# Sliding-window decode attention on one core: two engines' written-out orders become loops, transposes move ahead of the spread, the last values get banks of their own, and the last load is cut anew

## The chip, the cores and the metric

The kernel runs on one core of one Trainium2 chip. The metric is the device time of one execution in microseconds (us). Before the change the median of three runs is 183.75 us (183.66 to 183.91). The profiled execution, which all durations here come from, took 183.87 us, of which its span, from the first to the last instruction, is 182.6 us.

## The reference, cut to what matters

```python
B, Sq, D = 32, 1, 512;  Hq, Hkv, Sk, Dh = 32, 8, 2048, 128     # all bfloat16
W = 512                                   # the last 512 of 2048 cached positions
q = (x @ wq).reshape(B, Sq, Hq, Dh).transpose(0, 2, 1, 3)
k = repeat(k_cache[:, :, Sk - W:, :], 4, axis=1)                # each kv head serves 4 q heads
v = repeat(v_cache[:, :, Sk - W:, :], 4, axis=1)
p = softmax(einsum("bhqd,bhkd->bhqk", q, k) * Dh ** -0.5)
o = einsum("bhqk,bhkd->bhqd", p, v)
return o.transpose(0, 2, 1, 3).reshape(B, Sq, Hq * Dh) @ wo
```

Per core: 33.5 MB of keys, 33.5 MB of values and two weights of 4.2 MB are read, 75.5 MB in all, and 32 KB are written.

## The kernel before

The 32 batch rows are worked through in eight **quads** of four, numbered 0 to 7. One quad's keys (or values) are 4 MB, laid on 128 partitions, 32 KB on each; a partition is one (row, kv head, quarter of the window). Two buffers each hold keys (`K_sb`) and values (`V_sb`).

Every step has a letter, a quad and sometimes a part; the orders are written out with these names at the top of the file:

- **T** (VectorE, L516): transposes a quad's keys into `KT_sb`, in two halves, T.0 and T.1.
- **S** (TensorE, L346): the scores, half S.0 from T.0 and half S.1 from T.1.
- **M** (VectorE, L522 and L524): the maximum, negated. **X** (ScalarE, L565): the exponential with its sums. **N** (VectorE, L528 and L530): reciprocal and scaling, into `P_bf`.
- **E** (TensorE, L360): turns the probabilities to the layout of the values. **G** (ScalarE, L572): copies them out of PSUM into `PTc`.
- **B** (VectorE L536, ScalarE L578): the *spread*, `PTc` times a mask into `bd`, once for each of eight kv heads, shared out between the two engines.
- **P** (TensorE, L372): `bd` against the values, 32 groups of four matmuls, into four banks of PSUM, `O_ps`; "P7.0.18" is quad 7's groups 0 to 17.
- **C** (VectorE L541, ScalarE L583): *picks* four blocks out of those banks into `C_sb`. **F** (TensorE, L382) *folds* them, and **D** (ScalarE, L586) copies the fold into `o_sel`.
- **W** (TensorE, L467): `o_sel` times wo, 32 blocks, then two small copies and two stores.

What sets the order: each engine runs its steps in the written order (TensorE with a loop over three rounds of two quads, L440; VectorE and ScalarE unrolled, `DVE_OPS` and `ACT_OPS`), and `needs` gives each step the steps of other engines that it waits for. A P needs its spread, and the pick of the quad before, since `O_ps` is one set of banks. An N needs the X before it; an E needs its N. A fold F needs its pick. SyncE issues all loads in the order of `LOADS`; before a load into a buffer that is in use it waits for the T (keys, L250) or the pieces of P (values, L257) that read it last. wo goes into `K_sb` in three loads, W0, W1 and W2 (L265), of 22, 8 and 2 of its 32 blocks.

Around the change the order of the end is this:

```python
TAIL_OPS = "P7.0.18 P7.18.32 F6 F7"
DVE_OPS  = "... T6.0 M5 T6.1 N5 B5.0.4 C4.2.4 M6 T7.0 N6 T7.1 B6.0.4 C5.2.4 M7 N7 B7.0.5 C6.2.4 C7.2.4"
WOP      = [(0, 22), (22, 30), (30, 32)]
```

Of the kernel before, what the change touches and what calls it, by code (L numbers as in the profile page):

```python
# [19 lines left out]
S0.0 S0.1 S1.0 S1.1 E0 E1 P0.0.32  # L20
# [6 lines left out]
P7.0.18 P7.18.32 F6 F7  # L27
"""
ROUNDS = 3
DVE_OPS = """  # L30
T0.0 T0.1 T1.0 M0 T1.1 N0 M1 N1 B0.0.4 B1.0.4 T2.0 T2.1 M2 N2 B2.0.4 T3.0 T3.1 M3 N3 B3.0.4 T4.0
T4.1 M4 N4 B4.0.4 T5.0 C3.2.3 T5.1 C3.3.4 T6.0 M5 T6.1 N5 B5.0.4 C4.2.4 M6 T7.0 N6 T7.1 B6.0.4
C5.2.4 M7 N7 B7.0.5 C6.2.4 C7.2.4
"""
ACT_OPS = """
X0 X1 G0 B0.4.8 G1 B1.4.8 C0.0.4 X2 D0 G2 B2.4.8 C1.0.4 X3 D1 G3 B3.4.8 C2.0.4 X4 D2 G4 B4.4.8
C3.0.2 X5 D3 G5 B5.4.8 C4.0.2 X6 D4 G6 B6.4.8 C5.0.2 X7 D5 G7 B7.5.8 C6.0.2 C7.0.2 D6 D7
"""
# [7 lines left out]
WOP = [(0, 22), (22, 30), (30, 32)]  # L46

# [5 lines left out]
def bass_standalone__sliding_block_cached__sampling_kernel(  # L53
# [22 lines left out]
    NG = 4  # L76
# [7 lines left out]
    orders = {"PE": head + sum(rounds, []) + tail, "DVE": ops_of(DVE_OPS), "ACT": ops_of(ACT_OPS)}  # L84

    ends, total = {}, {}
    for eng, ops in orders.items():
        for op in ops:
            kind = op[0]
            key = ("ANY", "C") if kind == "C" else (eng, kind)  # L90
            total[key] = total.get(key, 0) + (op[3] - op[2] if kind == "C" else 1)
            if kind == "C":
                ends["C", op[1]] = key + (4 * op[1] + 4,)
            elif kind == "B":
                for i in range(op[2], op[3]):
                    ends[kind, op[1], i] = key + (total[key],)
            elif kind == "P":
                for g in range(op[2], op[3]):
                    ends["P", op[1], g] = key + (total[key],)
            elif kind == "D":  # L100
                ends[op] = key + (total[key] + 1,)
            else:
                ends[op] = key + (total[key],)

    def needs(op):
# [3 lines left out]
        if kind == "T":  # L109
            d = [("S", q - 1, op[2])]  # L110
        elif kind == "S":
            d = [("T", q, op[2]), ("X", q - 1)]
        elif kind == "M":
            d = [("S", q, 1)]
        elif kind == "X":
            d = [("M", q), ("N", q - 1)]
        elif kind == "N":
            d = [("X", q), ("E", q - 1)]
        elif kind == "E":
            d = [("N", q), ("G", q - 1)]  # L120
        elif kind == "G":
            d = [("E", q)] + spread(q - NG)
        elif kind == "B":
            d = [("G", q), ("P", q - 2, 31)]
        elif kind == "P":
            d = spread(q) + [("C", q - 1)]
        elif kind == "C":
            d = [("P", q, 31), ("F", q - 2)]
        elif kind == "F":
            d = [("C", q)]  # L130
        elif kind == "D":
            d = [("F", q)]
        return [ends[n] for n in d if n[1] >= 0]

    with ExitStack() as es:
# [3 lines left out]
        K_sb = [sb(f"K_sb{i}", [P, R * DH], BF16) for i in range(2)]  # L139
# [9 lines left out]
        PTc = sb("PTc", [P, NG, R, REP], BF16)  # L149
        C_sb = sb("C_sb", [P, 2, 4, DH], F32)  # L150
        o_sel = sb("o_sel", [P, NI, B], BF16)
# [3 lines left out]
        maxv = sb("maxv", [P, NQ], F32)  # L155
        negmax = sb("negmax", [P, NQ], F32)
        sums = sb("sums", [P, NQ], F32)
        recip = sb("recip", [P, NQ], F32)
# [10 lines left out]
        F_id = spare[:, 1280:1536].bitcast(F32).rearrange("p (r h) -> p r h", r=4)  # L169
        m_id = spare[:, 1536:1792].bitcast(F32).rearrange("p (b h k) -> p b h k", b=4, h=HKV)  # L170
        F_hd = spare[:, 1792:1856].bitcast(F32)
        m_red = spare[:, 1856:1920].bitcast(F32)
# [7 lines left out]
        S_ps, EP_ps, O_ps, F_ps, Y_ps = ps[:, 0], ps[:, 1], ps[:, 2:6], ps[:, 6], ps[:, 7]  # L180

        def folds(q):
            return (F_ps if q < NQ - 1 else S_ps)[:, 0:4 * NI]
# [57 lines left out]
        def _(sp):  # L241
            wait = Waits(sp)
            wo_h = wo.rearrange("(h r) n -> h (r n)", r=DH)
            wo_r = wo_h.rearrange("h (d m) -> h d m", d=4)
            for op in ops_of(" ".join(LOADS)):
                kind, q = op[0], op[1]
                if kind == "K":
                    if q >= 2:
# [13 lines left out]
                else:  # L262
                    wait([ends["T", NQ - 2, 1]])
                    i0, i1 = WOP[q]
                    sp.dma_start(  # L265
                        wo_sb[:, i0:i1, :].rearrange("p i n -> p (i n)"),
                        wo_r[:, :, i0 * D:i1 * D],
                    ).then_inc(sem_wo[q], 16)
# [3 lines left out]
        def _(pool):  # L272
# [10 lines left out]
            pool.sem_inc(op_sem["ACT", "D"], 1)  # L283
# [3 lines left out]
            diag(F_id[:, :, :], [[-32, 4], [-1, HQ]], "pool_f")  # L287
            diag(m_id[:, :, :, :], [[-32, 4], [-4, HKV], [-1, KB]], "pool_m")
# [30 lines left out]
        def _(pe):  # L319
# [48 lines left out]
            def pv(q, g0, g1):  # L368
                for g in range(g0, g1):
                    for b in range(4):  # L370
                        pr = slice(32 * b, 32 * b + 32)
                        ins = pe.matmul(  # L372
                            O_ps[:, b, :],
# [6 lines left out]
            def fold(q):  # L380
                for d in range(4):
# [3 lines left out]
                        rhs=C_sb[:, q % 2, :, NI * d:NI * d + NI],  # L385
# [11 lines left out]
            def waits_of(op):  # L397
# [3 lines left out]
                if kind == "S" and op[2] == 0:  # L401
                    yield ("ONE", "pool_qbd"), 4 * (q // 2) + 4
                    if q == 0:
                        yield ("ONE", "dve_q"), 4
                        yield ("ONE", "act_q"), 4
                elif kind == "E" and q == 0:
                    yield ("ONE", "pool_e"), 2
                elif kind == "F" and q < NQ - 1:
# [51 lines left out]
            for j, (i0, i1) in enumerate(WOP):  # L460
                pe.wait_ge(sem_wo[j], 16)
                last = j == len(WOP) - 1
                for cs in ((0, 1), (2, 3)) if last else (range(4),):
                    for i in range(i0, i1):
                        for c in cs:
# [3 lines left out]
                                lhsT=o_sel[:, i, :],  # L469
# [6 lines left out]
        def spread_args(q, h):  # L476
            return bd[:, q % 2, :, h, :], PTc[:, q % NG], mask[:, h:h + 1]

        def pick_args(q, r):
            pr = slice(32 * r, 32 * r + 32)  # L480
            return C_sb[pr, q % 2], O_ps[pr, :, r * DH:(r + 1) * DH]

        @block.vector
        def _(dve):
            wait = Waits(dve)
# [5 lines left out]
            dve.tensor_reduce(  # L491
                F_hd[:, :], F_id[:, :, :].rearrange("p r h -> p h r"), AX.X, ALU.add
            ).then_inc(s["dve_c"], 1)
            dve.wait_ge(s["pool_m"], 2)
            dve.tensor_reduce(
                m_red[:, :].rearrange("p (h k) -> p h k", h=HKV),
                m_id[:, :, :, :].rearrange("p b h k -> p h k b"), AX.X, ALU.add,
            ).then_inc(s["dve_c"], 1)
            dve.wait_ge(s["dve_c"], 2)
            dve.tensor_reduce(  # L500
                mask[:, :], m_red[:, :].rearrange("p (h k) -> p h k", h=HKV), AX.X, ALU.add
            ).then_inc(s["dve_c"], 1)
            for n in range(4):
                dve.wait_ge(s["pe_q"], 2 * n + 1)
                dve.tensor_copy(Q_row[:, 1024 * n:1024 * n + 512], ps[:, 2 * n]).then_inc(s["dve_q"], 1)  # L505
            dve.wait_ge(s["dve_q"], 4)
            dve.wait_ge(s["act_q"], 4)
# [6 lines left out]
            def turn(q, w):  # L514
                dve.wait_ge(sem_k[q % 2], 16 * (q // 2 + 1))
                return dve.transpose(  # L516
                    KT_sb[:, w].bitcast(F32).rearrange("p r c t -> p r (c t)"),
                    K_sb[q % 2][:, :].bitcast(F32).rearrange("p (r w c) -> p r w c", r=R, w=2)[:, :, w],
                )

            def maxes(q):
                dve.tensor_reduce(maxv[:, q:q + 1], S_ps, AX.X, ALU.max).then_inc(s["dve_m"], 1)  # L522
                dve.wait_ge(s["dve_m"], q + 1)
                return dve.tensor_scalar(  # L524
                    negmax[:, q:q + 1], maxv[:, q:q + 1], -SCALE, None, op0=ALU.mult)

            def norm(q):
                dve.reciprocal(recip[:, q:q + 1], sums[:, q:q + 1]).then_inc(s["dve_r"], 1)  # L528
                dve.wait_ge(s["dve_r"], q + 1)
                return dve.tensor_scalar(  # L530
                    P_bf[:, :], P_f32[:, :], recip[:, q:q + 1], None, op0=ALU.mult)

            def spread(q, h0, h1):
                for h in range(h0, h1):
                    o, i, m = spread_args(q, h)
                    ins = dve.tensor_scalar(o, i, m, None, op0=ALU.mult)  # L536
                return ins

            def pick(q, r0, r1):
                for r in range(r0, r1):  # L540
                    dve.tensor_copy(*pick_args(q, r)).then_inc(op_sem["ANY", "C"], 1)  # L541

            run = {"T": turn, "M": maxes, "N": norm, "B": spread, "C": pick}
            for op in orders["DVE"]:
                wait(needs(op))
                ins = run[op[0]](*op[1:])
                if ins:
                    ins.then_inc(op_sem["DVE", op[0]], 1)
# [4 lines left out]
        def _(act):  # L553
            wait = Waits(act)
            act.wait_ge(s["pool_j"], 1)
            act.activation(junk[:, 1:2], junk[:, 0:1], ACTF.Exp).then_inc(s["act_warm"], 1)
            for n in range(4):
                act.wait_ge(s["pe_q"], 2 * n + 2)
                act.activation(  # L559
                    Q_row[:, 1024 * n + 512:1024 * n + 1024], ps[:, 2 * n + 1], ACTF.Copy  # L560
                ).then_inc(s["act_q"], 1)
            act.wait_ge(s["dve_c"], 3)

            def exponential(q):
                return act.activation(  # L565
                    P_f32[:, :].rearrange("p (k r) -> p k r", k=KB),
                    S_ps.rearrange("p (r k) -> p k r", k=KB), ACTF.Exp,
                    bias=negmax[:, q:q + 1], scale=SCALE, accum_out=sums[:, q:q + 1],
                )

            def gather(q):
                return act.activation(  # L572
# [57 lines left out]
```

## Time and profile before

| what | us |
|---|---|
| median of three runs | 183.75 |
| profiled execution | 183.87 |
| its span | 182.6 |
| TensorE matmul busy | 118.9 |
| VectorE busy | 105.8 |
| ScalarE busy | 49.7 |
| GpSimd busy | 12.4 |

| group | instructions | mean ns |
|---|---|---|
| T, half a quad's keys, L516 | 16 | 4429 |
| P, one matmul, L372 | 1024 | 398 |
| S, one matmul, L346 | 256 | 527 |
| B on VectorE, one head, L536 | 33 | 349 |
| B on ScalarE, one head, L578 | 31 | 712 |
| C on VectorE, one block, L541 | 10 | 693 |
| C on ScalarE, one block, L583 | 22 | 589 |
| X, L565 | 8 | 689 |

How to read it: busy time is the time in which an engine worked on something; matmuls overlap, so four of 398 ns can be in flight and a new one starts every 55 ns or so. The DMA row of the page cuts the span into 40 slices and gives the busy share of the sixteen DMA engines in tenths. An instruction's idle time is put down to whatever ended it. The chain of waits goes back from the last instruction, at each step to what released it.

### The profile page before, as it was taken

How to read it: one execution, taken by the hardware profiler on the slowest of the kernel's cores; microseconds unless marked ns; L12 is line 12 of the kernel's file. 1: busy time of each engine (PE TensorE's matmuls, PEld its weight loads, DVE VectorE, ACT ScalarE, POOL GpSimd, SP SyncE). 2: the span in 40 equal slices, each digit the busy share in tenths (PEclk: the TensorE clock that was granted, in tenths of full speed). 3: DMA queues.
4: the chain of work that ended last, by engine and by line, in shares of the span. 5: the costliest groups of instructions: out<-in, count | busy, mean ns of one | idle time of the engine just before them, and what ended most of it. 6: DMA issues, size and time to landing. Idle time of an engine off the chain costs nothing.

```text
span 182.6 us, 3659 instructions
## 1 busy us (share of the span) xinstructions
PE 118.9 (65%) x1636; PEld 57.6 (32%) x1636; DVE 105.8 (58%) x101; ACT 49.7 (27%) x92; POOL 12.4 (7%) x34
## 2 busy tenths in 40 slices
PE   0029901425869898049954899334299869996984
PEld 0013300101535353015521453003035434552553
DVE  0031499999559713983279317999902799633030
ACT  3001300000490527402470107100106406443031
POOL 7400012000300000003000000003000000000000
PEclk9999995555769999756995589755559999999999
DMA  6999999999999999999999999999999999999991
GB/s 235 461 431 409 424 459 438 431 395 460 449 431 388 449 456 416 395 452 449 425 398 438 438 447 409 431 438 445 424 416 416 427 424 438 416 436 437 424 374 56
DMA packets 3461, 75.70 MB, mean 415 GB/s; under 512 B 412, under 2 KB 508, under 8 KB 636
## 3 DMA queue, kind: packets, MB, share of 16 engines
q1 hardware_dynamic: 3360, 75.52, 96.7%
q8 instruction: 7, 0.11, 0.3%
q10 hardware_dynamic: 92, 0.05, 0.1%
q14 instruction: 2, 0.02, 0.0%
HBM read 75.53 MB, written 0.03 MB: 414 GB/s over the span
## 4 chain that ended last, share of the span: by engine, by line
DMA 39%; PE 28%; DVE 25%; ACT 3%; issue 3%; SPq 0%; DVEq 0%
DVE KT_sb L516 20%; DMA K_sb<-in_k_cache_dram 16%; DMA V_sb<-in_v_cache_dram 16%; PE ps L372 16%; DMA V_sb<-in_wq_dram 7%; PE ps L334 5%; PE ps L346 3%; DVE QT_sb L508 2%; PE ps L360 2%; ACT bd L578 1%; PE ps L382 1%; DVE C_sb L541 1%; PE ps L467 1%; DVE maxv L522 1%; DVE bd L536 1%
## 5 line engine op out<-in xcount | busy, mean ns | idle before, releaser
L516 DVE STREAM_TRANSPOSE KT_sb<-K_sb 128x4096 f32<-128x4096 f32 x16 | 70.5, 4429 | 4.6 <-DMA K_sb<-in_k_cache_dram 4.5
L372 PE MATMUL ps<-V_sb,bd 32*128 32x512 bf16 x1024 | 62.7, 398 | 9.6 <-DMA V_sb<-in_v_cache_dram 6.5
L346 PE MATMUL ps<-KT_sb,QBD 128*32 128x512 bf16 x256 | 24.6, 527 | 36.2 <-DVE KT_sb L516 32.1
L372 PEld LDWEIGHTS ps<-V_sb,bd 32*128 32x128 bf16 x1024 | 27.0, 97 | 40.5 <-issue 9.8
L346 PEld LDWEIGHTS ps<-KT_sb,QBD 128*32 128x32 bf16 x256 | 6.6, 113 | 52.4 <-DVE KT_sb L516 35.4
L536 DVE TENSOR_SCALAR bd<-PTc,mask 128x512 bf16<-128x512 bf16 x33 | 9.4, 349 | 22.5 <-ACT PTc L572 22.5
L565 ACT ACTIVATE P_f<-ps,negmax 128x512 f32<-128x512 f32 x8 | 5.5, 689 | 58.0 <-DVE negmax L524 58.0
L578 ACT ACTIVATE bd<-PTc,mask 128x512 bf16<-128x512 bf16 x31 | 19.9, 712 | 0.3
L583 ACT ACTIVATE C_sb<-ps 32x512 f32<-32x512 f32 x22 | 13.0, 589 | 21.7 <-PE ps L372 21.4
L541 DVE COPY C_sb<-ps 32x512 f32<-32x512 f32 x10 | 6.9, 693 | 12.9 <-PE ps L372 12.7
L312 POOL COPY QBD<-QT_sb 32x256 bf16<-32x256 bf16 x16 | 6.3, 396 | 106.0 <-PE ps L346 91.2
L572 ACT ACTIVATE PTc<-ps 128x512 bf16<-128x512 f32 x8 | 4.8, 595 | 27.9 <-PE ps L360 27.9
L382 PE MATMUL ps<-C_sb,F_pad 128*128 128x128 f32 x64 | 12.0, 345 | 0.4 <-DVE C_sb L541 0.4
L382 PEld LDWEIGHTS ps<-C_sb,F_pad 128*128 128x128 f32 x64 | 10.2, 242 | 4.8 <-issue 2.9
L360 PE MATMUL ps<-P_bf,E_sb 128*128 128x128 bf16 x128 | 9.5, 233 | 2.2 <-DVE P_bf L530 2.2
L334 PE MATMUL ps<-V_sb,bd 128*128 128x512 bf16 x32 | 9.2, 459 | 1.9 <-DMA V_sb<-in_wq_dram 1.9
L360 PEld LDWEIGHTS ps<-P_bf,E_sb 128*128 128x128 bf16 x128 | 8.1, 105 | 6.3 <-issue 3.4
L522 DVE TENSOR_REDUCE maxv<-ps 128x1 f32<-128x512 f32 x8 | 5.5, 687 | 7.5 <-PE ps L346 7.5
L323 PE MATMUL ps<-bd 32*128 32x128 bf16 x4 | 0.6, 294 | 10.6 <-DMA bd<-in_x_dram 10.6
L487 DVE CAST bd<-ps 128x512 bf16<-128x512 f32 x1 | 0.7, 691 | 11.3 <-PE ps L323 11.3
L559 ACT ACTIVATE KT_sb<-ps 128x512 bf16<-128x512 f32 x4 | 2.4, 598 | 17.1 <-PE ps L334 17.1
L505 DVE CAST KT_sb<-ps 128x512 bf16<-128x512 f32 x4 | 2.8, 692 | 6.7 <-PE ps L334 6.7
(29 smaller groups left out, 31.0 us busy)
## 6 DMA issues: line engine op xcount, KB each, us to landing
K_sb<-in_k_cache_dram SPq DMA_DIRECT2D x8, 4096.0 KB, 24.6
V_sb<-in_v_cache_dram SPq DMA_DIRECT2D x5, 4096.0 KB, 29.4
V_sb<-in_v_cache_dram SPq DMA_DIRECT2D x4, 2048.0 KB, 21.0
V_sb<-in_wq_dram SPq DMA_DIRECT2D x1, 4096.0 KB, 12.3
K_sb<-in_wo_dram SPq DMA_DIRECT2D x1, 2816.0 KB, 20.9
V_sb<-in_v_cache_dram SPq DMA_DIRECT2D x1, 2304.0 KB, 13.1
V_sb<-in_v_cache_dram SPq DMA_DIRECT2D x1, 1792.0 KB, 14.8
K_sb<-in_wo_dram SPq DMA_DIRECT2D x1, 1024.0 KB, 22.7
```

The costliest lines, as they stand in the source:

```text
L312: pool.tensor_copy(QBD[pr].rearrange("p u a (h c) -> p u a h c", h=HKV).rearrange("p u (w t) h c -> p (u w) t h c", w=2)[:, :, :, :, 4 * b ...
L334: ins = pe.matmul(ps[:, n], lhsT=xT_sb[:, kt, :], rhs=wq_sb[:, kt, n * 512:(n + 1) * 512], start=kt == 0, stop=kt == DKT - 1, tile_positio ...
L346: ins = pe.matmul(S_ps[32 * c:32 * c + 32, :], lhsT=QBD[:, q % 2, 2 * w + t, c0:c0 + 32], rhs=KT_sb[:, w, :, KB * h:KB * h + KB, t], start ...
L360: ins = pe.matmul(EP_ps[:, e * R:(e + 1) * R], lhsT=window[:, KB - 1 - k:KB - 1 - k + P], rhs=P_bf[:, k * R:(k + 1) * R], start=k == 0, st ...
L372: ins = pe.matmul(O_ps[:, b, :], lhsT=bd[pr, q % 2, 4 * g:4 * g + 4].rearrange("p r h e -> p (r h e)"), rhs=V_sb[q % 2][pr, 512 * g:512 * ...
L382: ins = pe.matmul(folds(q), lhsT=F_sb[:, d].rearrange("p h d -> p (h d)"), rhs=C_sb[:, q % 2, :, NI * d:NI * d + NI], start=d == 0, stop=d ...
L516: return dve.transpose(KT_sb[:, w].bitcast(F32).rearrange("p r c t -> p r (c t)"), K_sb[q % 2][:, :].bitcast(F32).rearrange("p (r w c) -> ...
L522: dve.tensor_reduce(maxv[:, q:q + 1], S_ps, AX.X, ALU.max).then_inc(s["dve_m"], 1)
L536: ins = dve.tensor_scalar(o, i, m, None, op0=ALU.mult)
L541: dve.tensor_copy(*pick_args(q, r)).then_inc(op_sem["ANY", "C"], 1)
L578: ins = act.activation(o, i, ACTF.Copy, scale=m)
L583: act.activation(*pick_args(q, r), ACTF.Copy).then_inc(op_sem["ANY", "C"], 1)
```

## The change

Five things change together.

1. VectorE's and ScalarE's work on the quads is a loop over n = 0 to 7 with register values for the waits and for the buffer of `bd`, and with branches for what is not in every pass. The picks of quads 6 and 7 and the last folds stand behind the loop.
2. VectorE's order in one pass is: pick n-2, M n, N n, both halves of T n+1, then its half of spread n. Before, T n+1 stood partly ahead of N n and the spread n stood ahead of, or behind, T n+1 by hand. The spread is always four heads on each engine, and VectorE takes two of the four blocks of every pick (before, from quad 3 on).
3. TensorE's head is pipelined like the loop's body (E0 ahead of S1, E1 inside P0). In the tail, quad 7's P goes into four banks of its own, so it no longer waits for pick 6; the fold F6 stands between group 18 and the rest of P7.
4. wo's three loads hold 22528, 8704 and 1536 bytes of a partition instead of 22528, 8192 and 2048, and the last one is two loads, of 125 and of 3 partitions. The matmuls' cuts `WOP` stay.
5. Smaller: q is copied out of PSUM in four copies of 1024 columns instead of eight of 512; the mask takes one reduction instead of two; statistics and `PTc` are single-buffered; ScalarE waits for its own G before the spread; `o_sel` has eight columns more per block, so that the loop can write every fold at column 4n.

```diff
 HEAD_OPS = """
-S0.0 S0.1 S1.0 S1.1 E0 E1 P0.0.32
+S0.0 S0.1 E0 S1.0 S1.1 P0.0.12 E1 P0.12.16 P0.16.20 P0.20.32
 """
...
 TAIL_OPS = """
-P7.0.18 P7.18.32 F6 F7
+P7.0.12 P7.12.16 P7.16.18 F6 P7.18.32 F7
 """
...
+WO_LOADS = [(0, 11264), (11264, 15616), (15616, 16384, 125)]
...
+    for n in range(-1, NQ):
+        orders["DVE"] += (
+            ([("C", n - 2, 2, 4)] if n > 1 else [])
+            + ([("M", n), ("N", n)] if n >= 0 else [])
+            + ([("T", n + 1, 0), ("T", n + 1, 1)] if n < LAST else [])
+            + ([("B", n, 0, 4)] if n >= 0 else []))
...
         elif kind == "P":
-            d = spread(q) + [("C", q - 1)]
+            d = spread(q) + [("C", q - 1) if q < LAST else ("D", q - 2)]
...
+        def sums_of(b, q):
+            return ps[:, b if q < LAST else 4 + b]
...
-                    sp.dma_start(
-                        wo_sb[:, i0:i1, :].rearrange("p i n -> p (i n)"),
-                        wo_r[:, :, i0 * D:i1 * D],
-                    ).then_inc(sem_wo[q], 16)
+                    c0, c1, *cuts = WO_LOADS[q]
+                    for p0, p1 in zip([0] + cuts, cuts + [P]):
+                        sp.dma_start(
+                            wo_f[p0:p1, c0:c1], wo_p[p0:p1, c0:c1]
+                        ).then_inc(sem_wo[q], 16)
...
+            turn(0, 16)
+            with dve.Fori(0, NQ) as n:
+                odd = dve.snap(n % 2)
+                one = dve.snap(n + 1)
+                with dve.If(n > 1):
+                    dve.wait_ge(op_sem["PE", "P"], PIECES * n + 1)
+                    for r in (2, 3):
+                        dve.tensor_copy(*pick_args(r)).then_inc(op_sem["ANY", "C"], 1)
+                dve.wait_ge(op_sem["PE", "S"], 2 * n + 4)
...
+                dve.wait_ge(op_sem["ACT", "X"], one)
+                dve.reciprocal(recip[:, :], sums[:, :]).then_inc(s["dve_r"], 1)
...
+                with dve.If(odd):
+                    with dve.If(n < LAST):
+                        turn(0, 16 * (n // 2) + 32)
+                with dve.Else():
+                    turn(1, 16 * (n // 2) + 16)
+                dve.wait_ge(op_sem["ACT", "G"], one)
+                for h in range(4):
+                    ins = dve.tensor_scalar(
+                        bd[:, bass.ds(odd, 1), :, h, :].rearrange("p o r e -> p (o r) e"),
+                        PTc[:, :, :], mask[:, h:h + 1], None, op0=ALU.mult)
+                ins.then_inc(done("B"), 1)
```

## The prediction

> **What bounds the kernel now.** I read the page first. Two rows of it show a kernel that lives from its loads: nearly every slice of the DMA row is a 9, and the load queue's packets fill 96.7% of sixteen engines' span.
>
> ```profile
> DMA  6999999999999999999999999999999999999991
> q1 hardware_dynamic: 3360, 75.52, 96.7%
> DMA 39%; PE 28%; DVE 25%; ACT 3%; issue 3%; SPq 0%; DVEq 0%
> ```
>
> So a step in the middle costs something only if a load is issued too late. Next I read the load queue's own timeline (SyncE: start, duration): with the completions in the trace's records, each load is issued 6 us or more before the queue would run dry.
>
> ```profile
> 35.56 0.53 SPq L250 DMA_DIRECT2D K_sb<-in_k_cache_dram  x1
> 45.00 0.53 SPq L250 DMA_DIRECT2D K_sb<-in_k_cache_dram  x1
> 156.03 1.56 SPq L265 DMA_DIRECT2D K_sb<-in_wo_dram  x3
> ```
>
> K2, issued at 35.56, takes over when V0's first engine is done at 41.6; K3 (45.00) is wanted at 61; wo (156.03) at 168. That leaves the end. The chain of waits there (start, duration):
>
> ```profile
> 166.51 0.04 DVE C_sb L541
> 166.55 0.68 issue
> 167.23 0.71 DVE C_sb L541
> 167.94 0.24 issue
> 168.18 7.11 PE ps L372 x128
> ...
> 176.78 1.17 PE ps L382 x8
> ...
> 178.31 2.12 PE ps L467 x128
> ```
>
> P7 waits for pick 6 until 168.18, then pick 7, fold, copy, and W from 178.31. The DMA share in the last stretches (columns: stretch, length, PE, PEld, DVE, ACT, POOL busy, clock, DMA share, GB/s):
>
> ```profile
> 176.00:177.90 1.90, 1.47 (x12) 1.13 (x10) 0.70 (x2) 0.79 (x2) 0.00 (x0) 1.00 0.86 355
> 177.90:180.10 2.20, 1.83 (x125) 1.72 (x128) 0.00 (x0) 0.28 (x1) 0.00 (x0) 1.00 0.29 107
> ```
>
> The sixteen DMA engines end at different times: by the completion records W1's last comes at 179.40, 2.14 us behind its first at 177.26, and W2's at 180.02. W's blocks take 56 ns each (2.05 us / 128 x 4 is 64 ns with the gap; the starts are 56 ns apart), so block 30, the first of W2, could start at 178.31 + 30 x 0.056 = 179.99; it starts at 180.06. TensorE's chain and the loads thus end within 0.1 us of each other. **To gain, both must get shorter; to lose, one suffices.**
>
> **The change, part by part.** All against the profiled execution's 183.87 us, which stands 0.12 above the median.
>
> *Head.* The copies of q are 1024 wide: the last ScalarE one takes perhaps 0.4 longer (0.60 for 512 columns; an estimate between that and double), T0 ends 0.4 later, K2 goes out at 36.0, wanted 41.6. T1 now waits for N0: T0's end 35.9, S0.1 1.9, M to N 2.4 (row below), T1 8.8, so K3 goes out near 49 instead of 45, wanted 61. No cost; were the cover of 5 and 12 us gone, 0.4 and 4.
>
> *Middle.* T2 to T5 begin where keys land (52.85, 72.62, 92.26, 111.69), as before. Spread and VectorE's pick follow T, so P2 and P3 start about 0.8 later (T3 ends 81.42, spread 1.1, pick 1.4, fold 2.1, P2 at 86.1 against 85.31). V4 and V5 are issued behind K6 and K7, whose T4 and T5 end at 101.1 and 120.5 (121.39 before, with a pick between its halves). No load moves later, and P4 still waits for V4 (131.15). Cost 0.
>
> *T7 behind N6.* The rows of VectorE and TensorE:
>
> ```profile
> 144.05 0.69 DVE L522 TENSOR_REDUCE maxv<-ps 128x1 f32<-128x512 f32 x1 [0.43 <-PE ps L346]
> 144.85 4.43 DVE L516 STREAM_TRANSPOSE KT_sb<-K_sb 128x4096 f32<-128x4096 f32 x1
> 149.36 0.49 DVE L530 TENSOR_SCALAR P_bf<-P_f,recip 128x512 bf16<-128x512 f32 x1
> 154.12 1.10 DVE L536 TENSOR_SCALAR bd<-PTc,mask 128x512 bf16<-128x512 bf16 x4
> 157.17 1.16 PE L382 MATMUL ps<-C_sb,F_pad 128*128 128x128 f32 x8
> 159.22 0.49 DVE L530 TENSOR_SCALAR P_bf<-P_f,recip 128x512 bf16<-128x512 f32 x1
> ```
>
> Without a transpose between, M7's start to N7's end is 157.29 to 159.71, 2.42 us, so N6 ends at 144.05 + 2.42 = 146.47 instead of 149.85. P5 no longer stalls for E6 and ends near 154.2 instead of 155.4 (its second half waits for V5.1, landed 150.6). But T7 starts 1.55 later than its first half did and runs 8.77 in one piece (the pairs in the middle do): to 155.15 instead of 154.20. Queued behind it on VectorE: spread 6 (1.10) and pick 5 (1.42), to 157.65; fold 5 and P6 wait for that pick. Fold 5 starts at 157.70 instead of 157.17: **+0.53**.
>
> *P7 in own banks.* P6's last group would hand over at 161.97 + 4.43 = 166.40, now 166.93. P7 starts there and not at 168.18: **-1.25**. ScalarE's half of spread 7, now four heads, ends about 166.1 (E7 ends 162.6, G 0.6, its own wait and a register 0.2, four heads 2.6): covered by 0.8.
>
> *F6 inside P7.* 1.09 from the fold's start to the next matmul (157.17 to 158.26); it lay beside pick 7 (175.31 to 176.73): **+1.09**, and 0.05 for two switches. So pick 7 begins 0.1 earlier: -1.25 + 1.09 + 0.05 = -0.11. (The +0.53 is inside the -1.25.)
>
> *Registers and branches.* VectorE's trace has none; TensorE's loop does (duration min/median/max in ns):
>
> ```profile
> L440 PEldq ALU_OP  x3: 32/32/32, 92.1 to 164.8; - x3
> L440 PEldq COMPARE_BRANCH  x3: 76/213/243, 92.2 to 164.9; - x3
> ```
>
> A register operation with its gap is about 0.1 us, a branch taken 0.3. Between N6 and T7 stand one of those, a branch taken and another: 0.5. N6's own 0.49 may cover it all; so 0 to 0.5, and I take 0.2, nearer to covered, since in this trace VectorE's sequencer handles the wait behind spread 7 at 162.72, 0.02 after the first of its five instructions starts. The branches behind T7 have 8.8 us to hide in. W starts at 178.31 - 0.11 + 0.2 = 178.4. Below nothing: no row gives a gain.
>
> [...] In this trace TensorE's two taken branches cost 0.21 and 0.24 us, and after the second no fetch comes until 174.7.
>
> *wo's loads.* W1 carries 512 B more on each row, eight rows to an engine: 4 KB at 27 B/ns (32 KB in 1.213 us) is 0.15, so it lands at 179.55. Its eight blocks then end no earlier than 180.03, a floor 0.03 below today's 180.06. W2: a load of 25 rows of x shows how odd counts are spread (window 1.6 to 2.4 us; packets of the queue of x):
>
> ```profile
> DMA packets 44, 0.48 MB, mean 605 GB/s; under 512 B 5, under 2 KB 30, under 8 KB 30
> q10 hardware_dynamic: 30, 0.03, 16.4%
> ```
>
> 30 packets are 25 rows and 5 completions: five engines. 125 rows on five are 25 each, at about 0.062 us (between 46 ns for 1 KB and 84 for 2 KB): 1.55 us behind W1's end there, 177.41 plus that engine's lag. By packet times the five that carried x lag at most 0.3 to 1.3 us, giving 179.3 to 180.3. With all lags the bounds are 178.96 and 181.1. I take 179.6: covered.
>
> [...]
>
> *Sum.* W at 178.4, block 30 at 178.4 + 1.68 = 180.08 against 180.06: +0.02. Median 183.75 + 0.02, so **183.8 us**.
>
> **Rivals.**
> - *Branches are not hidden* (slower). Place: between N6 and T7, then spread 6 and pick 5. It decides once their overhead exceeds the 0.2 taken above by 0.35, so from 0.55 us on. Three branches taken (0.3 each) and eight register operations (0.1 each), all exposed, are 1.7; at 1.0, some of them hidden, W starts 0.8 later: 184.6. For: VectorE has never branched in this trace, so nothing shows that it prepares work behind a branch while it runs. Against: TensorE's prices, and the 0.49 and 8.8 us of work that stand ahead of the branches.
> - *W2 lands late on five engines* (slower). It decides from a lag of 1.1 + 0.35 on. At the largest, 2.14, W2 lands at 181.1: 184.8. For: half the engines lag. Against: the x engines seem to be early ones.
> - *The loads end earlier* (faster). By the packet records two 8 KB instruction fetches, at 90.0 and 109.3, kept a DMA engine for 0.31 to 0.33 us each; with short programs they go. If they hit the engine that sets W1, W1 lands 0.3 to 0.6 earlier. TensorE must then be as early: its granted clock is half until 137.0, so P4's first 48 matmuls take 5.31 us against 2.77 in P5, and a clock that returns sooner would bring S6, T7 and all behind them forward by up to 2.5. Both together give 183.75 - 0.03 - 0.6 = 183.1, one fetch 183.4. Against: the five largest lags arose at TensorE's own fetches (16 KB, 1.07 us, at 49.6, 60.6, 68.2, 85.4 and 95.1), and those stay.
> - *Code is fetched again at branches* (slower). A fetch of 16 KB takes 1.07 us in the packet records; one at each of three branches between N6 and pick 5 would add 3.2: 187. Against: TensorE's second jump back, at 140.6, is followed by none.
> - *The transposes' move does nothing* (no other time): where a T waits for its keys (T3, T4, T5), its order to N is idle. In the tail K7 has landed at 140.8, so there it acts.
>
> **How the numbers follow.** Forecast 0.48, branches exposed 0.20, W2 late 0.1, earlier loads 0.12, code fetched again 0.04, mixtures 0.06. That bound is 0.2%, 0.37 us, about what a measurement of this kernel can tell from no change. With 0.05 of the mixtures inside it: same 0.53, faster 0.12, slower 0.35. The forecast's own range is 183.6 (all registers hidden, W at the loads' floor, -0.03, and the median's own scatter of 0.1) to 184.1 (0.5 exposed). The whole range goes from 183.3, between one fetch and two, to 184.7, which takes in the branches at 1.0 and leaves out the worst lag of W2 and the fetches.
>
> **What would show it.** T7 should start near 146.5 and end near 155.3; P5 end near 154.2; fold 5 start near 157.8; P7 start near 167 without a wait; F6 stand between 171 and 172.5; W start near 178.4; W2 land before 180.1; no instruction fetch on the small queue after 0. A T7 that starts after 147, a W that waits for its last load, or any gap of 1 us in the DMA row would make this wrong.

## The result, and the profile after

The changed kernel takes 184.17 us (median of 22 runs, 183.73 to 184.39) against 183.67 for the kernel before on the same chips (22 runs). The ratio is 1.0027, with a 95% interval of 1.0021 to 1.0033: 0.50 us slower. That is inside the range on record, but beyond the 0.2% that I had called no change and held likeliest. The profiled execution took 184.26 us, with a span of 182.9.

The page of the changed kernel: the granted clock, the DMA row, the load queue, and the chain by engine.

```profile
PEclk9999975555559999965699589965589999999998
DMA  6999999999998999999999999999999999999981
q1 hardware_dynamic: 3352, 75.52, 96.7%
DMA 65%; DVE 14%; PE 9%; issue 8%; SPq 1%; DVEq 1%; ACT 1%; ACTq 0%
```

The loads are as full as before, and 75.52 MB are moved as before. The chain however goes through the loads to 65% instead of 39%. Its last part, in order of time (start, duration), says where:

```profile
155.57 24.61 DMA K_sb<-in_wo_dram
180.17 0.04 issue
180.22 0.81 PE ps L463 x40
181.03 0.02 issue
181.05 0.27 ACT P_bf L603
```

At the chain's end there is no pick, no fold and no VectorE any more, only a load of wo and 40 matmuls, W's last ten blocks, behind it. The timeline of the changed kernel's end, TensorE and VectorE (start, duration, engine, line, operation, shapes, and idle time before it with what ended it):

```profile
144.68 0.49 DVE L530 TENSOR_SCALAR P_bf<-P_f,recip 128x512 bf16<-128x512 f32 x1
145.15 8.77 DVE L507 STREAM_TRANSPOSE KT_sb<-K_sb 128x4096 f32<-128x4096 f32 x2
...
153.85 1.10 DVE L540 TENSOR_SCALAR bd<-PTc,mask 128x512 bf16 x4
...
154.98 1.42 DVE L519 COPY C_sb<-ps 32x512 f32<-32x512 f32 x2
...
156.46 1.16 PE L378 MATMUL ps<-C_sb,F_pad 128*128 128x128 f32 x8 [0.31 <-DVE C_sb L519]
...
166.07 4.07 PE L368 MATMUL ps<-V_sb,bd 32*128 32x512 bf16 x72 [0.33 <-DMA V_sb<-in_v_cache_dram]
170.07 1.16 PE L378 MATMUL ps<-C_sb,F_pad 128*128 128x128 f32 x8
171.16 3.20 PE L368 MATMUL ps<-V_sb,bd 32*128 32x512 bf16 x56
...
177.41 1.41 PE L463 MATMUL ps<-K_sb,o_sel 128*32 128x128 bf16 x88 [0.37 <-ACT o_sel L567]
180.22 0.74 PE L463 MATMUL ps<-K_sb,o_sel 128*32 128x128 bf16 x40 [1.40 <-DMA K_sb<-in_wo_dram]
180.99 0.28 DVE L549 CAST P_bf<-ps 64x128 bf16<-64x128 f32 x1 [5.17 <-PE ps L463]
```

TensorE reaches W at 177.41, 0.90 earlier than before (178.31), does W0's 22 blocks, and then stands for 1.40 us until W1 is there. The copies begin at 180.99 instead of 180.39, which is 0.60 later than in the kernel before:

```profile
180.39 0.28 DVE L550 CAST P_bf<-ps 64x128 bf16<-64x128 f32 x1 [3.66 <-PE ps L467]
```

A part comes back in the stores, which is not followed here; the profiled executions differ by 0.39 and the medians by 0.50.

The completion records of wo's loads (each load is complete on an engine when that engine has written its count; us from the span's start):

```
                         W1 first  W1 last   W2 last
before                     177.26   179.40    180.02
after                      177.59   180.17    180.40
```

I had put W1's last completion at 179.55. It came 0.62 later. W2 came at 180.40, while W1's eight blocks were still being multiplied, so W2 cost nothing. In the stretches of the changed kernel (columns: stretch, length, PE, PEld, DVE, ACT, POOL busy, clock, DMA share, GB/s) the loads' last 2.2 us are busier than before, 0.46 against 0.29, for little more data:

```profile
176.00:177.90 1.90, 1.53 (x44) 1.34 (x48) 0.00 (x0) 0.28 (x1) 0.00 (x0) 1.00 0.84 335
177.90:180.10 2.20, 0.92 (x68) 0.74 (x56) 0.00 (x0) 0.00 (x0) 0.00 (x0) 1.00 0.46 124
```

Busier at 124 GB/s instead of 107: single packets must have become slower. The packet records agree. W1's packets of 8704 bytes take 328 to 341 ns up to 177.5 (but for one of 865 right behind the 16 KB instruction fetch of 174.4), and 408 to 514 from 177.6 to the end; the last load's packets of 1536 bytes take 65 at first and 85 to 122 later.

### The profile page after: what moved, and what is told of

Read it like the earlier page. It is cut to its first block, busy times and chain, and to the rows that moved or that the text cites. A ratio compares the mean times of both kernels' runs of the same rounds, so it can differ in the third digit from the quotient of the medians.

```text
span 182.9 us, 3849 instructions
## 1 busy us (share of the span) xinstructions
PE 118.2 (65%) x1636; PEld 56.6 (31%) x1636; DVE 108.9 (60%) x103; ACT 46.6 (25%) x85; POOL 12.6 (7%) x34
## 3 DMA queue, kind: packets, MB, share of 16 engines
q1 hardware_dynamic: 3352, 75.52, 96.7%
## 4 chain that ended last, share of the span: by engine, by line
DMA 65%; DVE 14%; PE 9%; issue 8%; SPq 1%; DVEq 1%; ACT 1%; ACTq 0%
DMA K_sb<-in_k_cache_dram 29%; DMA V_sb<-in_v_cache_dram 16%; DMA K_sb<-in_wo_dram 13%; DVE KT_sb L507 11%; DMA V_sb<-in_wq_dram 7%; PE ps L330 5%; PE ps L368 2%; DVE QT_sb L495 2%; PE ps L342 1%; SPq L254 1%; ACT KT_sb L557 1%; PE ps L463 0%; DVE maxv L521 0%; SPq L263 0%; SPq L247 0%
## 5 line engine op out<-in xcount | busy, mean ns | idle before, releaser
L368 PE MATMUL ps<-V_sb,bd 32*128 32x512 bf16 x1024 | 64.1, 402 | 8.6 <-DMA V_sb<-in_v_cache_dram 8.5
L342 PE MATMUL ps<-KT_sb,QBD 128*32 128x512 bf16 x256 | 22.3, 486 | 32.1 <-DVE KT_sb L507 32.0
L368 PEld LDWEIGHTS ps<-V_sb,bd 32*128 32x128 bf16 x1024 | 26.4, 98 | 41.7 <-DMA V_sb<-in_v_cache_dram 9.3
L588 ACT ACTIVATE bd<-PTc,mask 128x512 bf16 x32 | 20.5, 710 | 1.4 <-ACT PTc L583 1.4
L540 DVE TENSOR_SCALAR bd<-PTc,mask 128x512 bf16 x32 | 8.9, 343 | 6.1 <-ACT PTc L583 6.1
L595 ACT ACTIVATE C_sb<-ps 32x512 f32<-32x512 f32 x14 | 8.2, 587 | 8.2 <-PE ps L368 8.0
L519 DVE COPY C_sb<-ps 32x512 f32<-32x512 f32 x12 | 8.3, 693 | 2.9 <-PE ps L368 2.6
L547 DVE COPY C_sb<-ps 32x512 f32<-32x512 f32 x4 | 2.8, 693 | 9.8 <-PE ps L368 9.7
L490 DVE CAST KT_sb<-ps 128x1024 bf16<-128x1024 f32 x2 | 2.4, 1224 | 7.3 <-PE ps L330 7.3
```

The source lines that it names most:

```text
L342: ins = pe.matmul(S_ps[32 * c:32 * c + 32, :], lhsT=QBD[:, q % 2, 2 * w + t, c0:c0 + 32], rhs=KT_sb[:, w, :, KB * h:KB * h + KB, t], start ...
L368: ins = pe.matmul(sums_of(b, q), lhsT=bd[pr, q % 2, 4 * g:4 * g + 4].rearrange("p r h e -> p (r h e)"), rhs=V_sb[q % 2][pr, 512 * g:512 * ...
L519: dve.tensor_copy(*pick_args(r)).then_inc(op_sem["ANY", "C"], 1)
L540: ins = dve.tensor_scalar(bd[:, bass.ds(odd, 1), :, h, :].rearrange("p o r e -> p (o r) e"), PTc[:, :, :], mask[:, h:h + 1], None, op0=ALU ...
L588: ins = act.activation(bd[:, bass.ds(odd, 1), :, h, :].rearrange("p o r e -> p (o r) e"), PTc[:, :, :], ACTF.Copy, scale=mask[:, h:h + 1])
L595: act.activation(*pick_args(r), ACTF.Copy).then_inc(op_sem["ANY", "C"], 1)
```

## The experiments

Two theories. **L**: the new cut of the last load costs it, since its rows on five DMA engines hold up W1 on the **late** engines, those that complete each load 1.5 us or more behind the first. **R**: the loops, the branches and the new order on VectorE and ScalarE cost it.

### The cuts alone, taken back and put in

The changed kernel with the old cuts:

```diff
-WO_LOADS = [(0, 11264), (11264, 15616), (15616, 16384, 125)]
+WO_LOADS = [(0, 11264), (11264, 15360), (15360, 16384)]
```

> The changed kernel with wo's three loads cut as before (22528, 8192 and 2048 bytes of a partition, 128 partitions each). Theory L (the new cut of the last load costs it: its rows on five DMA engines hold up W1 on the late engines, and ten of W's blocks wait for W1): W1 lands near 179.4, W2 near 180.0, W waits for W2 alone, its last two blocks start near 180.05; time as the kernel before, ratio 1.000 within 0.001. Theory R (the loops and the new order of VectorE and ScalarE cost it): the time stays that of the changed kernel, ratio 1.0027.

Measured: 183.77 us (11 runs) against 183.66, ratio 1.0003 (0.9994 to 1.0012). W1 completed at 179.43, W2 at 180.03. TensorE's rows for W, and VectorE's copy:

```profile
177.42 1.41 PE L463 MATMUL ps<-K_sb,o_sel 128*32 128x128 bf16 x88 [0.37 <-ACT o_sel L567]
179.47 0.90 PE L463 MATMUL ps<-K_sb,o_sel 128*32 128x128 bf16 x40 [0.65 <-DMA K_sb<-in_wo_dram]
180.41 0.28 DVE L549 CAST P_bf<-ps 64x128 bf16<-64x128 f32 x1 [4.57 <-PE ps L463]
```

W waited for W1 too (0.65), where I had expected it to wait for W2 alone. TensorE is as early as in the changed kernel (177.42), and the copy is where it was before the change (180.41 against 180.39). All of the loss is gone, and the loops, the transposes, the banks and the inserted fold together cost or save nothing that can be measured: what TensorE gains is spent waiting for the loads. Theory R falls.

The kernel before with the new cuts alone:

```diff
+WO_LOADS = [(0, 11264), (11264, 15616), (15616, 16384, 125)]
...
-                    i0, i1 = WOP[q]
-                    sp.dma_start(
-                        wo_sb[:, i0:i1, :].rearrange("p i n -> p (i n)"),
-                        wo_r[:, :, i0 * D:i1 * D],
-                    ).then_inc(sem_wo[q], 16)
+                    c0, c1, *cuts = WO_LOADS[q]
+                    for p0, p1 in zip([0] + cuts, cuts + [P]):
+                        sp.dma_start(
+                            wo_f[p0:p1, c0:c1], wo_p[p0:p1, c0:c1]
+                        ).then_inc(sem_wo[q], 16)
...
```

> The kernel before with nothing but the new cut of wo's loads (22528, 8704 and 1536 bytes, the last in 125 and 3 partitions). Theory L: W1 lands near 180.2 instead of 179.4, W's last ten blocks start there and the copies 0.6 later than before; ratio 1.0025 to 1.0035. Theory R: ratio 1.000 within 0.001.

Measured: 184.45 us (5 runs), ratio 1.0044 (1.0030 to 1.0059): the cuts alone bring the whole loss, and here somewhat more than expected. W1 completed at 180.04. TensorE's rows for W, matmuls and weight loads:

```profile
180.09 0.46 PEld L468 LDWEIGHTS ps<-K_sb,o_sel 128*32 128x32 bf16 x32 [0.60 <-DMA K_sb<-in_wo_dram]
180.09 0.99 PE L468 MATMUL ps<-K_sb,o_sel 128*32 128x128 bf16 x40 [0.43 <-DMA K_sb<-in_wo_dram]
180.77 0.13 PEld L468 LDWEIGHTS ps<-K_sb,o_sel 128*32 128x32 bf16 x8 [0.23 <-DMA K_sb<-in_wo_dram]
```

W waits twice, for W1 until 180.09 and for W2 until 180.77. The second wait is my rival "W2 lands late on five engines", which the changed kernel does not show. In this run some engines in the middle of the field lag (W0's completions lie 0.0 to 0.4, then 0.76, 1.10, 1.43 us and later behind the first); in the changed kernel nine others lie within 0.23 of the first, and after one at 0.5 come five at 1.7 to 2.0, six in W0. Two 8 KB instruction fetches, at 89.9 and 109.2, are in this run's packet records and not in the changed kernel's. Lags of 1.08 and 0.82 us appear in the key loads that complete right behind them (first completions at 90.3 and 109.7). That those fetches also make the difference in W2 is plausible and was not tried by itself.

### Boundary or split

The new cuts do two things: the second load grows by 512 bytes on each partition, and the last is split. The changed kernel without the split:

```diff
-WO_LOADS = [(0, 11264), (11264, 15616), (15616, 16384, 125)]
+WO_LOADS = [(0, 11264), (11264, 15616), (15616, 16384)]
```

> The changed kernel with its last load in one piece of 128 partitions; the boundaries (22528, 8704, 1536 bytes) stay. If the split into 125 and 3 partitions is what holds W1 up: W1 lands near 179.55, W2 near 180.0, ratio 1.000 within 0.001. If the larger second load is (8704 bytes instead of 8192): W1 still lands at 180.1 or later, ratio 1.002 or more. Theory R: ratio 1.0027.

Measured: 183.58 us (11 runs), ratio 1.0001 (0.9992 to 1.0010). W1 completed at 179.63 and W2 at 180.08, with the packets of W1 at 328 to 345 ns (again but for one of 865 behind the instruction fetch) and every one of the last load at 65 to 69.

```profile
177.47 1.41 PE L463 MATMUL ps<-K_sb,o_sel 128*32 128x128 bf16 x88 [0.37 <-ACT o_sel L567]
179.67 0.75 PE L463 MATMUL ps<-K_sb,o_sel 128*32 128x128 bf16 x40 [0.79 <-DMA K_sb<-in_wo_dram]
180.45 0.28 DVE L549 CAST P_bf<-ps 64x128 bf16<-64x128 f32 x1 [4.56 <-PE ps L463]
```

So it is the split. And my sum for the larger second load was near: I had 0.15 more, W1 came 0.20 later than with the old cuts (179.63 against 179.43), and nearly all of it stayed hidden (the copies begin at 180.45 instead of 180.41).

### Where the rows go

Why do five engines' small packets slow the other engines? Two theories. **Place**: which engines are slowed depends on the partitions that the rows are written to, so with the rows elsewhere W1 can land near the 179.63 of the run without the split. **Packets**: many small packets slow every other engine, wherever they are written. Two runs keep the source, the size and the count of the 125 rows, on five engines as before. They write them to the free key buffer, the one to low partitions and the other to high ones, and differ from each other in nothing else. Both leave most of wo's last two blocks out of its place, so their output is not the reference's:

```diff
+                    if q == 2:
+                        wait([ends["T", NQ - 1, 1]])
+                        sp.dma_start(
+                            K_sb[1][0:25, 0:5 * 768].rearrange("p (a n) -> p a n", a=5),
+                            wo_p[0:125, c0:c1].rearrange("(p a) n -> p a n", a=5),
+                        ).then_inc(sem_wo[q], 16)
+                        sp.dma_start(wo_f[125:128, c0:c1], wo_p[125:128, c0:c1]).then_inc(sem_wo[q], 16)
+                        continue
```

> The changed kernel, but the 125 rows of the last load go, five to a partition, to partitions 0 to 24 of the free key buffer instead of to their 125 places; source, packet size, count and the five engines stay, and W's last two blocks are computed from what the buffer held, so the output lacks them. [...] Theory packets (five engines with many small packets slow every other engine, wherever they write): W1 lands near 180.2 with packets of 400 to 510 ns, as in the changed kernel.

The other run writes to `K_sb[1][64:89, ...]`.

> As the run with the rows on partitions 0 to 24, but on partitions 64 to 88; the output lacks the same. [...] Theory packets: near 180.2, as with partitions 0 to 24.

Measured, one execution each: 184.64 us with the rows on partitions 0 to 24 and 184.82 with them on 64 to 88, which two single executions do not tell apart. The traces do. W1 completed at 180.41 with the rows on partitions 0 to 24, and at 180.71 with them on 64 to 88. TensorE's wait for W1 in the one and in the other:

```profile
180.45 0.74 PE L471 MATMUL ps<-K_sb,o_sel 128*32 128x128 bf16 x40 [1.13 <-DMA K_sb<-in_wo_dram]
```

```profile
180.76 0.74 PE L471 MATMUL ps<-K_sb,o_sel 128*32 128x128 bf16 x40 [1.63 <-DMA K_sb<-in_wo_dram]
```

By its last completion the low run missed the 179.63 of the run without the split. The engines one by one say more (completion records; lag behind the first engine, in us, of the six latest; the records do not name the engines, so W0 and W1 are matched by the order of the lags):

```
                         in W0                                in W1
rows in place (after)    1.68 1.69 1.73 1.83 1.84 1.95        2.01 2.26 2.38 2.47 2.48 2.58
rows uncut               1.54 1.55 1.59 1.65 1.68 2.03        1.51 1.54 1.56 1.58 1.68 2.02
rows on 0 to 24          1.58 1.59 1.82 1.95 2.00 2.12        1.56 1.58 1.80 1.98 2.12 2.95
rows on 64 to 88         1.59 1.65 1.80 1.87 1.96 2.12        2.29 2.66 2.93 3.02 3.27 3.32
```

With the rows on 0 to 24, five of the six late engines keep their lag as if there were no such rows, and one falls back by 0.8 to 1.0. With the rows on 64 to 88, all six fall back, by 0.7 to 1.3. The packets of 178.0 to 178.4 us fit:

```
                     8704 bytes: ns min median max    1536 bytes: ns min median max
rows uncut           328  332  336                    (none in this stretch; 65 to 69 elsewhere)
rows on 0 to 24      328  328  608                     65   65  153
rows in place        465  474  514                     89  106  113
rows on 64 to 88     547  560  564                    106  120  136
```

Theory packets gives one and the same picture for both, and falls: in these two executions the partition written to decides. Why one late engine was held up by the rows on 0 to 24 as well, neither run shows. What a slowed large packet and a small one move together can be estimated, if one small packet runs beside each large one (the records name neither engine nor partition). In the high run, 8704 bytes in 560 ns and 1536 in 120 make 15.5 + 12.8 = 28 bytes per ns; in the low run, the slowest of each, 608 and 153 ns, make 14.3 + 10.0 = 24. That is about the 26.5 of one large packet alone (8704 in 328 ns). What limits the two together, and which partitions it concerns, no run here shows.

### A smaller last load

With the loads' end fixed, only what stands behind them can shrink. The changed kernel with an uncut last load of one block:

```diff
-WOP = [(0, 22), (22, 30), (30, 32)]
-WO_LOADS = [(0, 11264), (11264, 15616), (15616, 16384, 125)]
+WOP = [(0, 22), (22, 31), (31, 32)]
+WO_LOADS = [(0, 11264), (11264, 15872), (15872, 16384)]
```

> The changed kernel with wo's loads uncut and a last load of one block (22528, 9216 and 1024 bytes), and the matmuls cut to match (22, 9 and 1 blocks). Theory L, with the loads' end fixed at 180.0: four matmuls instead of eight start behind it, 0.06 us less than with the old cuts, ratio 0.999 to 1.000 against the kernel before. If a smaller last load ends later by its own cost, 1.000 to 1.001. Theory R: 1.002 or more.

Measured: 183.72 us (11 runs), ratio 1.0006 (0.9997 to 1.0015). That is no gain that can be measured, as the 0.06 expected would hardly be. None of the runs was measurably faster than the kernel before.

## Why the prediction was right or wrong

- **What bounds the kernel.** Right, and it decided: "to gain, both must get shorter; to lose, one suffices". TensorE's chain was 0.90 shorter and nothing came of it; the loads' chain got longer, and that showed. Hardly any of the 0.90 is the change's own, though, as the third point says.
- **Head and middle.** Right. K2 went out at 36.27 (forecast 36.0), K3 at 49.51 (49), K7 at 120.52 (120.5), and the DMA row has no hole.
- **T7 behind N6.** Right in the working: N6's end and T7's start are one point, T7 runs 8.77, spread, pick and fold follow without gaps, and P5 ends at 154.2. The start of it all was off: S6 and M6 came 1.37 earlier. TensorE's granted clock returned to full at 134.09, not 137.00, so P4's first 48 matmuls took 4.19 us instead of 5.31 (before and after):

```profile
131.15 5.31 PE L372 MATMUL ps<-V_sb,bd 32*128 32x512 bf16 x48 [5.83 <-DMA V_sb<-in_v_cache_dram]
```

```profile
131.18 4.19 PE L368 MATMUL ps<-V_sb,bd 32*128 32x512 bf16 x48 [6.08 <-DMA V_sb<-in_v_cache_dram]
```

  I had this as part of the faster rival. In the other profiles the clock's return is at 133.9, 134.2, 135.8, 136.1 and 136.2 in versions of the changed kernel and at 136.9 in the version of the kernel before. P4 starts at 131.0 to 131.2 in all eight, so the return came 2.7 to 5.9 us after P4's first matmul (2.92 in the changed kernel, 5.85 before); what sets the moment, no run shows. By the clock's records of the two kernels' profiles, every stretch between two changes is a whole multiple of 3.41 us: 3.41 to 20.48 before, 6.83 to 47.79 after. The mean granted clock of the executions of the changed kernel alone goes from 0.81 to 0.84; so the early return looks like luck of the profiled execution, which no run tried by itself. Where the clock returned at 136.21 (the last load of one block), S6 and W start so:

```profile
141.69 1.91 PE L342 MATMUL ps<-KT_sb,QBD 128*32 128x512 bf16 x32
177.87 1.41 PE L463 MATMUL ps<-K_sb,o_sel 128*32 128x128 bf16 x88 [0.37 <-ACT o_sel L567]
```

  S6 starts 0.39 earlier than before (142.08) and W 0.44. What is left for the reordering itself is 0.05, near the 0.11 that the prediction had for quad 7's own banks and F6 together.
- **P7 in own banks, F6 inside it.** Right: P7 no longer waits for a pick (a new wait of 0.33 for V7.0 appears), and F6 takes 1.09 of TensorE's time (170.07 to 171.16).
- **Registers and branches.** I took 0.2 of 0 to 0.5; it was 0. VectorE's trace now has them (duration min/median/max in ns), here those of the jump ahead of T:

```profile
L534 DVEq COMPARE_BRANCH  x7: 43/47/63, 53.7 to 158.6; - x7
```

  In the pass before T7 the register operation and the first branch are recorded at 144.71 and 144.80 and the last preparation ends at 145.11, all while N6 runs (144.68 to 145.17). The rival "branches are not hidden" is out, and so is "code is fetched again": after the start the packet records hold seven fetches of 16 KB, as many as before, which I take for TensorE's, and none of 8 KB.
- **wo's loads.** This is the step that failed, in "so it lands at 179.55" and in "I take 179.6: covered". For W2 I had counted the time of the five engines that carry it, and for W1 its own bytes alone. That the rows of the one could slow the packets of the other on other engines was in neither bound. W1 landed at 180.17, 0.62 later than the step's 179.55, and ten blocks of W stand behind W1 where two stand behind W2: 0.60 at the copies. The packet time was too small as well: I took 0.062 us for each of W2's rows on the five engines, and 65 ns is what they took at first, but 85 to 122 later. So W2 came at 180.40 and not at 179.6; it cost nothing only because W1 was late too.
- **The likeliest case.** "No change" (0.53) was wrong, "slower" had 0.35. The rival that I gave for a late last load has the right load and the wrong place: what W waited for was not W2 on the five engines that carry it, but W1 on the late engines, at 180.17. That the time still lies in the whole range (183.3 to 184.7) is luck: its upper end came from exposed branches, which cost nothing, and the forecast's own range ended at 184.1. W itself was forecast for 178.4 and began at 177.41, an error of the other sign that the loads hid.

## What to carry to other kernels

When loads set the end, check when each DMA engine finishes, and not only when the last one does; a gap of 2 us between them (2.14 in W1 before) looks like room, but putting W2's rows on five engines brought nothing in earlier here: W1 came at 180.17 instead of 179.63, W2 at 180.40 instead of 180.08. A load that is split over engines another way can slow a load in front of it (W1's packets took up to 514 ns instead of 328), so ask what is multiplied behind *that* one. And before a chain of compute is shortened, check what lands last: here TensorE was 0.9 us earlier, and that was worth nothing.

## What was not expected of the hardware

- How much the rows of a split load slowed the packets of the load in front of it went with the partitions they were written to: at 178.0 to 178.4 us the median of an 8704-byte packet was 332 ns without the split, 328 with the rows on partitions 0 to 24, 474 with them in place and 560 with them on 64 to 88. By the estimate above a slowed one and a small one move 24 to 28 bytes per ns together, against 26.5 for a large one alone.
- An instruction fetch of 16 KB (1.06 to 1.10 us for the first five by the packet records; I take them for TensorE's) seems to leave its DMA engine late for the rest of the run: in the changed kernel the 32 KB packet right behind each of the first five took 1.67 to 1.71 us where the median is 1.21, and five lags of 1.7 to 2.0 us appear in the completion records one by one after the fetches at 48.9, 60.9, 70.7, 89.1 and 96.1 and are as large in the last load of V; a sixth comes with the fetch at 174.4.
- A branch on VectorE took 43 to 69 ns, and the one ahead of T7 ran while the instruction before it was still at work (144.80, N6 to 145.17).
- TensorE's granted clock changed only at distances of whole multiples of 3.41 us, in the profiles of both kernels (3.41 to 20.48 us before, 6.83 to 47.79 after).
